# Thresholded attention with a gated MLP: scores in row tiles, probabilities turned by VectorE, values in 64x64 tiles

## The chip, the cores and the metric

The kernel runs on one core of a Trainium2 chip. The metric is the device time of one execution in microseconds (us), as the median of several runs. TensorE (PE) multiplies matrices into PSUM, VectorE (DVE), ScalarE (ACT) and GpSimd (POOL) work on elements, and SyncE (SP) issues all transfers.

## The reference

Eight batches of eight heads, 576 positions, 64 elements per head. Each row of scores keeps only what lies within tau (0.02) of its maximum; the result of attention goes, with heads side by side, through a gated MLP.

```python
scores = scale * np.matmul(q, k.transpose(0, 1, 3, 2))
thresh = np.max(scores, axis=-1, keepdims=True) - tau
scores = np.where(scores >= thresh, scores, -1000000000.0)
scores = scores - np.max(scores, axis=-1, keepdims=True)
attn = np.exp(scores)
attn = attn / (np.sum(attn, axis=-1, keepdims=True) + 1e-09)
x = np.matmul(attn, v)                      # then (B, S, H * D)
...
h = gelu(x @ w_in)                          # 512 -> 1024, halves u and v
v_s = np.einsum('ts,bsd->btd', w_sg, layernorm(v) * g_ln) + b_sg[None, :, None]
out = x + (u * v_s) @ w_out
```

## The kernel before

The unit of work is a pair of heads, n = 0 to 31, four pairs to a batch. In SBUF the two heads of a pair lie on partitions 0 to 63 and 64 to 127. The 576 query rows of a head are four tiles of 128 and a tail of 64; the two tails of a pair share one tile (i = NM = 4). So a pair has nine tiles of scores, each 128 rows by 576 columns in two PSUM banks.

Scores are wanted more exactly than one pass of the f32r form gives, so q and k are split in a high part and a rest (`hi_part`, L590; the rests at L595 and L624). DMAs inside SBUF (`k_place` L608, `k_place_lo` L616, `q_place` L630) then stack these parts on all 128 partitions, so that one full matmul of 288 columns adds two products at once (`scores`, L692): 4 matmuls per tile, 6 for the tail tile. Pair 0 has no split: its scores run in f32, two heads side by side as 64-row tiles of the array (`whole_scores`, L674).

For each tile DVE takes the negative maximum (`maxima`, L701), POOL the threshold (L707), ACT Exp out of PSUM (`exponentials`, L727), and DVE multiplies that by "score at least threshold" and sums the row on the way (`select`, L734). Then the tile of probabilities has to be turned, since values contract over keys. From pair 4 on, tiles i = 0 and 1 of both heads are turned in 32x32 squares by DVE (`turn_squares`, L830), written to DRAM in one transfer (`sqd`, L835) and read back in four (L840). All other tiles, and all tiles of pairs 0 to 3, are turned by PE against an identity (L415, for the tail L879 with `both`), and ACT copies them from PSUM into place (L870, L890, L892).

Values (`values`, L907) run in f32, which the profile counts as two passes per matmul, for 256 query columns (p = 0) and 320 (p = 1): per part five key tiles for each head, into the partitions of that head, as two column tiles 128x64 of the array. DVE multiplies by the reciprocals of the row sums (L916), ACT and POOL split the result for the MLP (L921, L923, L925). The reciprocals are spread through DRAM too (`ird`, L768 to L781).

The MLP's matmuls (L1017, and L1033 for batch 0) lie between those of the pairs. Every step is a function in a list, `plan`; the table `ORDER` gives the sequence in which the steps are issued, and so the sequence on each engine and in SP's one queue of transfers. `PLACES` gives the PSUM bank for each use. Buffers are named by tags: a tag with a number is one buffer that is used again once its last reader is done.

## Time and profile before

| | us |
|---|---|
| median of 3 runs (923.26 to 924.45) | 923.83 |
| span of the profiled execution | 919.5 |
| PE busy | 894.3 (97%) |
| DVE busy | 736.1 (80%) |
| ACT busy | 586.3 (64%) |
| POOL busy | 584.3 (64%) |
| DMA, 172.10 MB | 65.6% of 16 engines on SP's queue |

The span runs from the first to the last instruction of the profiled execution; 4.3 us of the median lie outside of it. A row of a group says how many instructions of one line there are, how long they were busy together, the mean of one in ns, and the idle time of the engine ahead of them with what ended it. Matmuls are pipelined: the mean of one is longer than the distance from one start to the next, and so prices of matmuls are read from start to start in the timeline.

### The profile page before, as it was taken

To read this page: it belongs to the slowest core of one execution; us is meant where nothing else is said; L and a number is where in the kernel's file an instruction comes from. 1 tells how busy PE (TensorE), PEld (TensorE's weight loads), DVE (VectorE), ACT (ScalarE), POOL (GpSimd) and SP (SyncE) were. 2 spreads that over 40 slices of the span, in tenths; PEclk is the share of its full clock that TensorE was granted. 3 is DMA by queue.
4 is the path that set the end of the run, shared out by engine and by line. 5 is a ranking of instruction groups with operands and counts; after the bars stand their busy time and mean duration, and the time that the engine had idled before them with its cause. 6 is when DMAs were issued, how large, how long until landed. Compare 5 with 4: busy or idle time off the path is not lost.

```text
span 919.5 us, 19187 instructions
## 1 busy us (share of the span) xinstructions
PE 894.3 (97%) x6281; PEld 761.4 (83%) x6281; DVE 736.1 (80%) x1605; ACT 586.3 (64%) x1197; POOL 584.3 (64%) x1095
## 2 busy tenths in 40 slices
PE   8989887999999999999999999999999999999998
PEld 5657675889788988988789888888889888899898
DVE  6987999877988779887898679977798778876254
ACT  5787767656676477754685557665686647763361
POOL 5476777656775487655685667764686557754373
PEclk9999989999999999999999999999999999999999
DMA  7776567686866776777767687676777776554001
GB/s 235 207 199 187 157 175 204 193 243 201 233 195 192 210 212 195 213 212 204 218 166 221 189 248 197 187 217 187 217 197 199 216 220 205 150 166 143 20 1 59
DMA packets 93981, 172.10 MB, mean 187 GB/s; under 512 B 25401, under 2 KB 41529, under 8 KB 90298
## 3 DMA queue, kind: packets, MB, share of 16 engines
q1 hardware_dynamic: 93882, 170.88, 65.6%
q8 instruction: 50, 0.82, 0.4%
q14 instruction: 49, 0.40, 0.2%
HBM read 80.61 MB, written 43.48 MB: 135 GB/s over the span
## 4 chain that ended last, share of the span: by engine, by line
PE 74%; DVE 11%; issue 4%; ACT 3%; DMA 3%; POOL 2%; SPq 2%; DVEq 0%; POOLq 0%; ACTq 0%
PE all_banks L1017 40%; PE all_banks L692 14%; PE all_banks L907 12%; PE all_banks L415 7%; DVE nm L701 3%; DVE p L734 3%; DVE sq L830 1%; ACT p L727 1%; DMA rk<-in_kT 1%; DMA ir<-ird 1%; ACT pt L870 1%; DVE gt L1002 1%; DMA klz<-klo 1%; POOL ot L1232 1%; PE all_banks L879 0%
## 5 line engine op out<-in xcount | busy, mean ns | idle before, releaser
L727 ACT ACTIVATE p<-all_banks,nm 128x576 f32<-128x576 f32 x256 | 186.1, 739 | 114.2 <-DVE nm L701 113.0
L701 DVE TENSOR_REDUCE nm<-all_banks 128x1 f32<-128x576 f32 x288 | 210.0, 745 | 45.3 <-PE all_banks L692 37.5
L734 DVE SCALAR_TENSOR_TENSOR p<-all_banks,nm,p 128x576 f32<-128x576 f32 x256 | 203.2, 808 | 39.3 <-ACT p L727 21.2
L692 PE MATMUL all_banks<-ks,qst 128*128 128x288 f32 x620 | 174.4, 314 | 6.0 <-DVE p L734 4.0
L707 POOL TENSOR_TENSOR nm<-columns,nm 128x1 f32<-128x1 f32 x288 | 57.8, 207 | 161.0 <-DVE nm L701 138.1
L907 PE MATMUL all_banks<-pt,rv 128*64 128x256 f32 (+1 forms) x1152 | 151.5, 408 | 0.0
L692 PE MATMUL all_banks<-klz,qst 128*128 128x288 f32 x496 | 138.3, 296 | 0.0
L692 PEld LDWEIGHTS all_banks<-ks,qst 128*128 128x128 f32 x620 | 113.6, 189 | 27.2 <-DVE p L734 15.1
L907 PEld LDWEIGHTS all_banks<-pt,rv 128*64 128x64 f32 x1152 | 77.8, 137 | 54.3 <-issue 5.9
L870 ACT ACTIVATE pt<-all_banks 128x512 f32<-128x512 f32 (+1 forms) x208 | 102.5, 534 | 19.0 <-PE all_banks L415 17.8
L1232 POOL TENSOR_TENSOR ot<-ot,x 128x288 f32<-128x288 f32 x112 | 90.6, 811 | 35.2 <-ACT ot L1241 30.3
L1017 PE MATMUL all_banks<-wsh,z 128*128 128x288 f32 (+2 forms) x512 | 111.8, 298 | 0.3 <-DVE ir L916 0.3
L1017 PE MATMUL all_banks<-x,wi 128*128 128x288 f32 (+2 forms) x720 | 111.7, 299 | 0.0
L415 PE MATMUL all_banks<-ident_r,p 128*128 128x128 f32 x648 | 98.4, 278 | 11.0 <-DVE p L734 8.2
L1017 PE MATMUL all_banks<-wi,x 128*128 128x512 f32 (+1 forms) x424 | 108.8, 401 | 0.0
L1017 PE MATMUL all_banks<-gh,wo 128*128 128x288 f32 (+1 forms) x480 | 106.0, 299 | 0.1
L1017 PEld LDWEIGHTS all_banks<-x,wi 128*128 128x128 f32 x720 | 99.7, 188 | 2.7 <-issue 0.9
L692 PEld LDWEIGHTS all_banks<-klz,qst 128*128 128x128 f32 x496 | 94.0, 189 | 1.0
L415 PEld LDWEIGHTS all_banks<-ident_r,p 128*128 128x128 f32 x648 | 77.4, 143 | 20.5 <-DVE p L734 9.9
L1017 PEld LDWEIGHTS all_banks<-wi,x 128*128 128x128 f32 (+1 forms) x424 | 75.5, 186 | 18.4 <-issue 0.9
L1017 PEld LDWEIGHTS all_banks<-wsh,z 128*128 128x128 f32 x512 | 84.5, 189 | 2.9 <-DVE uu L996 1.1
L830 DVE STREAM_TRANSPOSE sq<-p 128x512 f32<-128x512 f32 (+1 forms) x112 | 82.0, 757 | 0.4
(201 smaller groups left out, 1719.8 us busy)
## 6 DMA issues: line engine op xcount, KB each, us to landing
sqd<-sq SPq DMA_DIRECT2D x28, 1152.0 KB
pt<-sqd SPq DMA_DIRECT2D x112, 288.0 KB
rk<-in_kT SPq DMA_DIRECT2D x32, 320.0 KB
rv<-in_vP SPq DMA_DIRECT2D x32, 320.0 KB
ks<-khi SPq DMA_DIRECT2D x62, 160.0 KB
rq<-in_qT SPq DMA_DIRECT2D x32, 288.0 KB
qst<-qhi SPq DMA_DIRECT2D x62, 144.0 KB
qst<-rq SPq DMA_DIRECT2D x62, 144.0 KB
```

Of the source, the lines that this page charges most:

```text
L415: nc.tensor.transpose(out, x, ident_r.bitcast(F32))
L692: nc.tensor.matmul(sc[:, a, 0:HALF], w, x, start=(j == 0), stop=(j == len(terms) - 1))
L701: nc.vector.tensor_reduce(nmax, st["s", h, i][:, :, 0:HALF], AX.XY, ALU.max, negate=True)
L707: nc.gpsimd.tensor_tensor(thr, toff, st["nm", h, i], ALU.subtract)
L727: nc.scalar.activation(target(h, i), st["s", h, i][:, :, 0:HALF], AF.Exp, bias=st["nm", h, i])
L734: nc.vector.scalar_tensor_tensor(dst, st["s", h, i][:, :, 0:HALF], st["thr", h, i], dst, ALU.is_ge, ALU.mult, accum_out=st["l", p][:, c:c ...
L830: nc.vector.transpose(st["sqt"][:, i, :, m0:m1], src)
L870: nc.scalar.activation(dst, src, AF.Copy)
L907: nc.tensor.matmul(acc[h * D:(h + 1) * D, 0:w], st["v"][:, o:o + D], x, start=(kt == 0), stop=(kt == NM))
L1002: put("stt1", end, lambda: nc.vector.scalar_tensor_tensor(t["tmp"], t["tmp"], GELU_C, t["acc"], ALU.add, ALU.mult))
L1017: nc.tensor.matmul(st["acc"][0:rows[0]] if rows else st["acc"], w, x, start=(j == 0), stop=(j == n - 1))
L1232: return lambda: nc.gpsimd.tensor_tensor(o(), o(), x[b, m][:, ts_], ALU.add)
```

## The change

Six things change together.

1. Scores: for tiles 0 to 3 every pair multiplies the two heads as two 64-row tiles of the array, three products (qh·kh, qh·kl, ql·kh) instead of a stack. That is 12 matmuls for two tiles and 48 per pair. The tail keeps 6 full matmuls, against `qz`, which holds both heads' tails with zeros between. The DMAs that stacked q and k are gone.
2. Select: ACT takes max(s − thr, alpha·(s − thr)) with alpha = BIG (Prelu, from PSUM), then Exp in place in SBUF, with the row sums as a by-product. DVE has no select; POOL makes the threshold and the bias of Exp for two heads in one small operation each.
3. Turning: DVE turns all nine tiles in 32x32 blocks. PE's transposes and ACT's copies are gone, from pair 0 on.
4. Exchange: blocks keep one half where they are; the other goes through DRAM and comes back on other partitions: three puts and three gets for tiles 0 and 1 (u = 0, pieces of 512 bytes), and again for the rest (u = 1, 640 bytes).
5. Values: 64x64 tiles of the array, 9 chunks of keys x 2 heads x 2 halves of rows, 128 columns for u = 0 and 160 for u = 1, into two banks. The result is scaled in two operations for all 576 columns and split in one each.
6. Reciprocals go out in three transfers and come back in four; v is loaded in another layout, 576 KB per pair instead of 320; there are ten buffers for single tiles of probabilities instead of two for double ones and `pm`; `ORDER` and `PLACES` are new. The MLP's own functions change only in how they are entered into the plan.

```diff
-                        terms = [(q[h][:, qo:qo + P], k[:, ko:ko + HALF]) for k in (st["ks", h], st["kl", h])]
...
+                terms = [("q", "k")] if whole_s else [("qh", "kh"), ("qh", "kl"), ("ql", "kh")]
+                for j, (q, k) in enumerate(terms):
+                    for a in range(2):
+                        for h in range(2):
+                            rows = slice(h * D, (h + 1) * D)
+                            nc.tensor.matmul(st["s", h, i][:, a, 0:HALF], st[q][rows, i * P:(i + 1) * P],
+                                             st[k][rows, a * HALF:(a + 1) * HALF], start=(j == 0), stop=(j == len(terms) - 1))
...
-                nc.scalar.activation(target(h, i), st["s", h, i][:, :, 0:HALF], AF.Exp, bias=st["nm", h, i])
...
-                nc.vector.scalar_tensor_tensor(dst, st["s", h, i][:, :, 0:HALF], st["thr", h, i], dst,
-                                               ALU.is_ge, ALU.mult, accum_out=st["l", p][:, c:c + 1])
...
+            tag = slot("p", PBUFS)
...
+                nc.scalar.activation(halves(st["p", h, i]), st["s", h, i][:, :, 0:HALF], AF.Prelu,
+                                     bias=columns_of(i)[1][:, h:h + 1], alpha=BIG)
...
+            return lambda: nc.scalar.activation(st["p", h, i], st["p", h, i], AF.Exp, bias=columns_of(i)[2][:, h:h + 1],
+                                                accum_out=l_of[part][:, c:c + 1])
...
+        def turn_blocks(h, i):
+            def f():
+                u = 0 if i < 2 else 1
+                t, w = turned(u).rearrange("p c e w -> p (c e) w"), WIDTHS[u] // 2
+                if i == NM:
+                    out = t.rearrange("p j (h w) -> p j h w", h=2)[:, :, :, w - HB:w]
+                else:
+                    out = t[:, :, h * w + i % 2 * BLK:h * w + (i % 2 + 1) * BLK]
+                nc.vector.transpose(out, st["p", h, i].rearrange("p (j x) -> p j x", x=BLK))
...
+        def put_blocks(u, k):
...
+                to, rows, e = ((slice(0, 2 * BLK), MIDDLE, 0), (slice(2 * BLK, 3 * BLK), FIRST, 1), (FINAL, FINAL, 1))[k]
+                nc.sync.dma_start(st["sw", u][to].rearrange("p (c w) -> p c w", c=PAIRS), turned(u)[rows, :, e])
...
+        def get_blocks(u, k):
...
+                nc.sync.dma_start(turned(u)[rows, :, e], st["sw", u][src].rearrange("p (c w) -> p c w", c=PAIRS))
...
+                for c in range(PAIRS):
+                    for h in range(2):
+                        for r in range(2):
+                            rows = slice(r * D, (r + 1) * D)
+                            nc.tensor.matmul(st["acc"][h * D:(h + 1) * D, r, :, c0:c0 + w], v[rows, c, h],
+                                             turned(u)[rows, c, :, h * w:(h + 1) * w], start=(c == 0), stop=(c == PAIRS - 1))
```

The order on three engines, in the middle of the program. Numbers at the end of a name tell buffers apart.

On PE before, the scores of a tile (L692) lie among products of the MLP (L1017) and the transposes of tiles that were finished earlier (L415, L879):

```order
L692 MATMUL all_banks<-ks_0_4039,qst_116 128x288
L692 MATMUL all_banks<-klz_123,qst_116 128x288
L692 MATMUL all_banks<-ks_0_4039,qst_116 128x288
L692 MATMUL all_banks<-klz_123,qst_116 128x288
L415 MATMUL all_banks<-ident_r,p_3_4118 128x128 x5
L879 MATMUL all_banks<-both,pm 128x64
L415 MATMUL all_banks<-ident_r,pm 128x128 x4
L1017 MATMUL all_banks<-wi_357,x_3018 128x512 x3
```

On PE after, the scores of a row tile of both heads (L592), both values groups of the pair before (L715), and the next pair's first scores:

```order
L592 MATMUL all_banks<-kh_3507,qh_3580 128x288 x4
L592 MATMUL all_banks<-kl_3590,qh_3580 128x288 x4
L592 MATMUL all_banks<-kh_3507,ql_3745 128x288 x4
L715 MATMUL all_banks<-pt_10_3651,rv_3804 64x2x64 x36
L715 MATMUL all_banks<-pt_10_3755,rv_3804 64x2x80 x36
L592 MATMUL all_banks<-kh_3831,qh_3869 128x288 x4
L592 MATMUL all_banks<-kl_3896,qh_3869 128x288 x4
L592 MATMUL all_banks<-kh_3831,ql_3898 128x288 x4
L809 MATMUL all_banks<-wi_412,x_3389 128x512 x3
```

No transposes stand between any more, and the two values groups follow each other.

On ACT before, Exp (L727) and the copies of turned tiles (L870, L890) take turns with splits and the MLP:

```order
L727 ACTIVATE p_2_4053<-all_banks,nm_1_2_4078 128x576
L727 ACTIVATE pm<-all_banks,nm_0_4_4081 128x576
L1241 ACTIVATE ot_1_0_4116<-all_banks 128x288
L727 ACTIVATE p_3_4118<-all_banks,nm_1_3_4114 128x576
L870 ACTIVATE pt_1_4138<-all_banks 128x4x128
L727 ACTIVATE p_3_4118<-all_banks,nm_0_3_4128 128x576
L921 ACTIVATE x_4141<-ir_0_3809 128x256
L890 ACTIVATE tt_4200<-all_banks 128x128
L870 ACTIVATE pt_1_4138<-all_banks 128x4x128
L921 ACTIVATE x_4141<-ir_1_3900 128x320
```

On ACT after, a Prelu (L628) and an Exp (L634) per tile:

```order
L628 ACTIVATE p_1_0_4188<-all_banks,columns 128x576
L628 ACTIVATE p_0_0_4190<-all_banks,columns 128x576
L1026 ACTIVATE ot_1_0_4198<-all_banks 128x288
L543 ACTIVATE kh_4217<-rk_4041 128x576
L628 ACTIVATE p_0_1_4219<-all_banks,columns 128x576
L634 ACTIVATE p_0_0_4190,l_120<-p_0_0_4190,columns 128x576
L628 ACTIVATE p_1_1_4233<-all_banks,columns 128x576
L634 ACTIVATE p_1_0_4188,l_120<-p_1_0_4188,columns 128x576
L634 ACTIVATE p_1_1_4233,l_120<-p_1_1_4233,columns 128x576
L634 ACTIVATE p_0_1_4219,l_120<-p_0_1_4219,columns 128x576
```

Both tiles of a head pair are selected before the first of them is exponentiated; the copies are gone.

In SP's queue before, the placing transfers of the next pair (L608, L616, L630) lie between the square put (L835) and its gets (L840):

```order
L835 DMA sqd_1943<-sq_1904 128x2304
L608 DMA ks_1_2061<-khi_1977 64x640 x2
L608 DMA ks_0_2064<-khi_1977 64x576 x2
L616 DMA klz_123<-klo_2015 64x576
L584 DMA rq_2068<-in_qT 128x576
L840 DMA pt_0_2070<-sqd_1943 32x4x576
L616 DMA klz_124<-klo_2015 64x576
L768 DMA ird_1_2155<-ir_1_2102 4x32x32
L768 DMA ird_0_2157<-ir_0_2105 4x32x32
L584 DMA rk_2159<-in_kT 128x640
L840 DMA pt_0_2070<-sqd_1943 32x4x576
```

In SP's queue after, the puts of the second part (`swb`, L695), the reciprocals' puts (L656), the gets of the first part (`swa`, L702) and of the second:

```order
L695 DMA swb_2660<-pt_7_2609 288x1x160
L695 DMA swb_2660<-pt_7_2609 576x1x160
L695 DMA swb_2660<-pt_7_2609 288x1x160
L656 DMA ird_2686<-ir_2680 32x32
L702 DMA pt_7_2518<-swa_2641 32x9x128
L702 DMA pt_7_2518<-swa_2641 64x9x128
L656 DMA ird_2686<-ir_2680 32x32
L702 DMA pt_7_2518<-swa_2641 32x9x128
L656 DMA ird_2686<-ir_2680 2x32x32
L702 DMA pt_7_2609<-swb_2660 32x9x160
L702 DMA pt_7_2609<-swb_2660 64x9x160
L702 DMA pt_7_2609<-swb_2660 32x9x160
```

The gets of both parts now stand directly behind the puts of the second part and among the reciprocals.

## Rows read from the trace of the kernel before

**Rows 1.** The page: busy time, the chain that ended last, one group

```profile
PE 894.3 (97%) x6281; PEld 761.4 (83%) x6281; DVE 736.1 (80%) x1605; ACT 586.3 (64%) x1197; POOL 584.3 (64%) x1095
...
PE 74%; DVE 11%; issue 4%; ACT 3%; DMA 3%; POOL 2%; SPq 2%; DVEq 0%; POOLq 0%; ACTq 0%
...
L870 ACT ACTIVATE pt<-all_banks 128x512 f32<-128x512 f32 (+1 forms) x208 | 102.5, 534 | 19.0 <-PE all_banks L415 17.8
```

**Rows 2.** Windows: stretch, its us, PE, PEld, DVE, ACT, POOL, PE clock, DMA, GB/s

```profile
80.00:120.00 40.00, 36.48 (x235) 28.54 (x234) 37.93 (x79) 28.79 (x55) 28.09 (x49) 0.96 0.61 175
240.00:360.00 120.00, 119.90 (x860) 103.05 (x859) 100.10 (x218) 80.03 (x163) 80.52 (x153) 1.00 0.75 211
```

**Rows 3.** Windows, the matmuls of L907 alone: us, PE, PEld, PE clock, DMA, GB/s

```profile
240.00:360.00 120.00, 23.32 (x180) 12.19 (x180) 1.00 0.75 211
```

**Rows 4.** Groups by form on PE: count, busy us, mean ns, idle before

```profile
L415 PE MATMUL all_banks<-ident_r,p 128*128 128x128 f32 x648 | 98.4, 278 | 11.0 <-DVE p L734 8.2 <-ACT tt L890 1.3 <-DVE pm L734 0.9
```

**Rows 5.** Timeline of PE (start, us, instruction, count): four transposes

```profile
408.20 0.60 PE L415 MATMUL all_banks<-ident_r,p 128*128 128x128 f32 x4
408.56 0.38 PE L1017 MATMUL all_banks<-gl,wo 128*128 128x288 f32 x1
408.77 0.43 PE L1017 MATMUL all_banks<-gh,wo 128*128 128x288 f32 x2
409.04 0.30 PE L1017 MATMUL all_banks<-gl,wo 128*128 128x288 f32 x1
```

**Rows 6.** Timeline of PE: the scores of a row tile in pair 0

```profile
16.16 1.24 PE L674 MATMUL all_banks<-rk,rq 64*128 64x288 f32 x8
17.33 0.66 PE L415 MATMUL all_banks<-ident_r,p 128*128 128x128 f32 x4
```

**Rows 7.** Timeline of PE: both values groups of pair 0

```profile
22.80 2.38 PE L907 MATMUL all_banks<-pt,rv 128*64 128x256 f32 x20
25.11 0.48 PE L1261 MATMUL all_banks<-warm 128*128 128x256 f32 x1
...
36.68 2.37 PE L907 MATMUL all_banks<-pt,rv 128*64 128x320 f32 x16
38.88 0.71 PE L907 MATMUL all_banks<-tt,rv 128*64 128x320 f32 x4
```

**Rows 8.** Timeline of PE, cut from 23.05 to 23.064, and to 23.073

```profile
22.80 0.44 PE L907 MATMUL all_banks<-pt,rv 128*64 128x256 f32 x2
...
22.80 0.65 PE L907 MATMUL all_banks<-pt,rv 128*64 128x256 f32 x4
```

**Rows 9.** Timeline of PE: the last score ahead of a values group

```profile
416.21 0.29 PE L692 MATMUL all_banks<-klz,qst 128*128 128x288 f32 x1
416.43 1.30 PE L907 MATMUL all_banks<-pt,rv 128*64 128x320 f32 x8
```

**Rows 10.** Groups by form on DVE: count, busy, mean ns, idle before

```profile
L701 DVE TENSOR_REDUCE nm<-all_banks 128x1 f32<-128x576 f32 x288 | 210.0, 745 | 45.3 <-PE all_banks L692 37.5 <-ACT pt L870 3.0 <-PE all_banks L674 2.2
L734 DVE SCALAR_TENSOR_TENSOR p<-all_banks,nm,p 128x576 f32<-128x576 f32 x256 | 203.2, 808 | 39.3 <-ACT p L727 21.2 <-POOL nm L707 13.0 <-ACT tt L890 1.3
L830 DVE STREAM_TRANSPOSE sq<-p 128x640 f32<-128x640 f32 x56 | 45.4, 822 | 0.4
L830 DVE STREAM_TRANSPOSE sq<-p 128x512 f32<-128x512 f32 x56 | 38.5, 693 | 0.0
```

**Rows 11.** Timeline of ACT: two Exp one behind the other

```profile
241.68 0.73 ACT L727 ACTIVATE p<-all_banks,nm 128x576 f32<-128x576 f32 x1
242.31 0.74 ACT L727 ACTIVATE pm<-all_banks,nm 128x576 f32<-128x576 f32 x1
```

**Rows 12.** Groups by form on ACT: an operation with two pointers

```profile
L1126 ACT ACTIVATE vv<-vv,bn 128x512 f32<-128x512 f32 x32 | 25.9, 809 | 5.4 <-POOL bn L1122 5.4
```

**Rows 13.** Timeline of SyncE's DMA queue: a square put and the gets behind it

```profile
833.92 0.33 SPq L835 DMA_DIRECT2D sqd<-sq  x1
838.05 1.74 SPq L840 DMA_DIRECT2D pt<-sqd  x4
```

More of the change, by code (lines that the diff above doesn't have):

```diff
@@ L508, in weights, with from_single @@
         for k, job in enumerate(jobs):
-            group = (f"w{sum(k >= first for first in (NC, 2 * NC, 2 * NC + NM + 2))}", "first")
-            job(lambda kind, time, fn, group=group: at(kind, time, fn, group), 1.0 + 1.9 * k, k)
-    def from_single(src, hi, lo, put, time, k):
+            job(lambda kind, fn, k=k: at(kind, k, fn), k)
+    def from_single(src, hi, lo, put, k):
         t, sp = {}, spare()
@@ L1101, in new @@
                 return st["v", i]
-            gelu2(put, end, acc, new, f"{b}_{i}", i == NM, part)
+            gelu2(put, acc, new, f"{b}_{i}", i == NM, part)
             def stats():
```

715 lines of the change are left out of this document (258 added, 457 removed), and 445 rows, old and new, of the table ORDER.

## The prediction, on record before the changed kernel ran

> **What bounds the kernel now.** I read the page first: TensorE (PE) is busy for 894.3 of 919.5 us and holds 74% of the chain that ended last; VectorE (DVE) comes next with 80% busy and 11% of the chain [rows 1]. Then the windows, to see whether one limit holds throughout. From 240 to 360 us PE is busy for 119.90 of 120 us, at the full granted clock, with DVE at 100.10, ScalarE (ACT) at 80.03, GpSimd (POOL) at 80.52 and the DMA engines at 0.75. From 80 to 120 us PE has 36.48 of 40, but DVE 37.93: there the first pairs wait for DVE [rows 2]. 180 passes of values lie in those 120 us, 40 to a pair: 4.5 pairs, 26.7 us each [rows 3]. A busy share says nothing of how densely matmuls follow each other, so I went on to start-to-start times. Pricing all matmuls of that stretch by the times below gives about 115.5 of 120 us, so 0.965 of a steady stretch is work that a removed matmul gives back. The time is therefore predicted as PE work removed per pair (n from 8 to 31), DVE work removed in the start, and a look at who might become late instead.
>
> **PE, removed.** Row tiles 0 and 1 of each pair from n=4 on already go by the square exchange; the others still take 22 transposes per pair, all 648 with one shape [rows 4]. From 408.20 to 408.77 us lie four of them and one product; two products take 0.27 us (408.77 to 409.04), so 0.135 each, and the four take 0.435, or 0.109 each [rows 5]. 22 x 0.109 = 2.40, with two passes of L879 as long as a product (0.16 together, an estimate): **2.56 us per pair** gone.
>
> **PE, scores.** 38 full matmuls of 288 columns become 48 half-height ones and 6 full ones. If the two heads' row tiles run side by side, the 48 take 24 slots, together 30: 8 x 0.135 = **1.06 us** gone. Row tiles do run so in pair 0, which already has them: eight f32 passes of 288 columns take 16.16 to 17.33, 0.146 each or 0.51 ns per column [rows 6], close to the 0.43 to 0.45 of the column tiles below, of which two run at once.
>
> **PE, values.** Today: 20 passes of 256 columns from 22.80 to 25.11, 2.31 us, and 20 of 320 columns at (38.88 − 36.68)/16 = 0.1375, 2.75 us; 5.06 per pair [rows 7]. They run as two column tiles at once: a cut of the timeline from 23.05 to 23.064 shows two passes, one to 23.073 four, so both partners of the next slot start within 9 ns [rows 8]. Afterwards there are 72 passes of 128 columns and 72 of 160, in four 64x64 tiles. If four run at once, that is 18 slots of each kind. A slot of 128 columns is half of what two column tiles take for 256 (0.231/2 = 0.1155), one of 160 is 0.1375: 18 x 0.253 = 4.55, **0.5 us** gone.
>
> **PE, added.** Where PE changes between full array and tiles, it loses something: 416.21 to 416.43 is 0.22 for a score before values, against 0.135 [rows 9]; about 0.09 per change. Counted in the order of both kernels, the changed one has 8.9 such changes per pair, the old one 3.4: **0.5 us** more. Net 2.56 + 1.06 + 0.5 − 0.5 = 3.62 per pair; 24 pairs give 87, by 0.965 **90 us**.
>
> **DVE and the start.** Per pair DVE loses nine selects (0.808) and four long transposes (two at 0.822, two at 0.693), and gains nine transposes of 576 columns, between those two, 0.757: 9 x (0.745 + 0.808) + 3.03 = 17.0 becomes 9 x (0.745 + 0.757) = 13.5 [rows 10]. For pairs 4 to 7, where DVE is the limit, that is 4 x 3.5 = 14, of which I take 13 as the tile work beside it has pitches somewhat shorter than these durations; pairs 0 to 3 have no long transposes now and change little, 2. Sum: 90 + 13 + 2 = **105 us** off the profiled execution.
>
> **ACT.** It takes over the select: per tile a Prelu from PSUM and an Exp in place of one Exp from PSUM, of which two follow each other after 0.63 us [rows 11]. Neither new form is in this trace. For the Prelu I take the same 0.63. For the Exp in place, with its sum: at least 0.63 too, at most 0.81, what 512 columns with two pointers take [rows 12]; I take 0.78, near the upper row, since it also has two pointers. In the steady stretch ACT is busy 80.03 / 4.5 = 17.8 per pair; nine Exp go from that (5.7) and the placing of transposed tiles (102.5 over 32 pairs, 3.2) [rows 1 to 3], nine times 1.41 = 12.7 comes: 21.6. PE will need 26.7 − 3.62 / 0.965 = 22.9. ACT stays hidden, but by little more than one us, and becomes the second engine in place of DVE. POOL loses the select's zeros and gains the two-column steps; it stays near 580.
>
> **The exchange.** The placing copies of k and q (1.5 MB per pair) and the square exchange go; the new one moves 2.65 MB per pair in pieces of 512 and 640 B, six puts and six gets. One 1152 KB put now lands 838.05 − 833.92 = 4.1 us after its issue, and four gets take 1.74 us to issue [rows 13]. A pair's last chain, score to values, is then: two maxima 1.5, two Prelu 1.26, two Exp 1.56, two transposes 1.51, three puts at 0.33 and 4.1 to land, three gets 1.3 and at most 4.1 to land: 16.3 us, some of it overlapped, but without queueing. In the changed order the PE work between a pair's last score and its second values group, priced by the rows above, is mostly 17 to 20 us (14.3 at the least). So it fits, with a thin margin; cost taken: nothing. If queueing adds more, PE, which works in order, waits at the values: 1 us per pair costs about 28 over the pairs from 4 on.
>
> **Sum.** 919.5 − 105 = 814.5. The median of 923.83 lies 4.3 above the span, and I keep that: **819 us**.
>
> **Rivals.**
> (a) The exchange is late. SP issues all transfers in one queue; a get that waits for its put also holds the loads behind it. For it: the margin of a few us, where a put issued behind a waiting get adds its whole wait. Against: ten of today's placing transfers per pair leave the same queue. At 2 us per pair 819 + 56 = 875; from 3.7 us per pair the gain is gone and it ends above 923.
> (b) Four 64x64 tiles don't run at once. Each pass brings its own small weights; if PE can feed only two tiles at a time, four passes take as long as two slots one after the other, and values cost 9.1 instead of 4.55: +4.55 x 31 / 0.965 = 146, **965 us**, slower than before. It decides from where four passes cost over 1.7 times a slot: 105 us are 3.3 per pair. Against it: partners start within a few ns of each other [rows 8]. The Trainium skill, "TensorE: Matmul & The Clock Gate", section "Wait — 56ns, not 53.3ns?", says that with hardware decode off each MATMUL costs some 62 ns of its sequencer. By that rule four passes would need 0.248 us for a slot of 0.1155, 36 x 0.248 = 8.9 us per pair (an estimate), and the time would be near 960. The trace speaks against that rule here, since two matmuls that start within 9 ns cannot each have taken 62 [rows 8].
> (c) The row tiles of the scores don't overlap, so that the change doesn't do what it says there: +24 x 0.135 = 3.24 per pair, 819 + 27 x 3.24 / 0.965 = 910 if the first five pairs hide it, as DVE does now.
> (d) ACT becomes the bound. For it: by the sum above it has 1.3 us per pair to spare. It decides from Prelu and Exp together at 1.41 + 1.3 / 9 = 1.55 us per tile, which the upper ends, 0.63 + 0.81, don't reach; at 1.7 it gives 9 x 0.15 x 27 = 36 more, 855.
> (e) The short pieces make the DMA engines the bound. Bytes fall, pieces multiply; at half of today's rate 2.65 MB cost 19 us, and with the loads some 24, over PE's 22.9: 819 + 27 x 1.1 = 849.
> (f) Better than the sum: the changes of mode cost less, PE's waits for DVE shrink: 778.
>
> **How the numbers follow.** Forecast 0.53 (789 to 847, within 1 us of lateness per pair), (f) 0.06, (a) 0.20 of which 0.05 above 923, (b) 0.06, (c) 0.04, (d) 0.07, (e) 0.04. The range goes from 784, below which half of (f) lies, to 890: it leaves out (b), most of (c), the end of (a), together no more than 0.2. Slower by over 0.2% (about what this measurement can tell from no change): (b) 0.06 and (a) 0.05, 0.11; within 0.2%: 0.01; faster: 0.88.
>
> **What the profile of the changed kernel would show.** Right: PE still above 95% in the middle and the largest part of the chain; eighteen slots of values in about 2.1 and 2.5 us; twelve score matmuls of a row tile in 0.8 us; DVE near 610 and ACT near 700 busy; no wait of the values on transfers above half a us. Wrong: PE idle before the values with a DMA as releaser (a); a values group of 36 program matmuls above 4 us (b); twelve scores in 1.6 us (c); Prelu and Exp above 1.55 us per tile (d); 512 B pieces at half the rate (e).

## The result and the profile after

The changed kernel takes **914.55 us** (median of 4 runs, 914.04 to 916.05), the one before, run beside it, 924.01 us: ratio 0.990, 95% interval 0.989 to 0.992. It is faster, but by 9.5 us where 105 were forecast, and it lies outside the range of 784 to 890. The profiled execution has a span of 914.3 us.

The page of the kernel after: busy time, the clock granted to TensorE in 40 slices, the chain that ended last.

```profile
PE 827.9 (91%) x9260; PEld 717.7 (78%) x9260; DVE 644.7 (71%) x1142; ACT 684.5 (75%) x1425; POOL 598.2 (65%) x1053
...
PEclk9897989999989999999899999999999999999999
...
PE 40%; POOL 16%; DVE 12%; DMA 11%; SPq 9%; ACT 8%; issue 6%; DVEq 0%; POOLq 0%; ACTq 0%
```

Against [rows 1], PE has lost 66 us of busy time and is still at 91%, but it holds 40% of the chain instead of 74%: the rest is shared by five others, none above 16%. Windows of the kernel after (stretch, its us, PE, PEld, DVE, ACT, POOL, PE clock, DMA, GB/s), the same stretches as [rows 2]:

```profile
80.00:120.00 40.00, 35.47 (x421) 28.88 (x422) 32.35 (x52) 30.53 (x61) 23.80 (x38) 0.86 0.78 205
240.00:360.00 120.00, 109.77 (x1214) 97.11 (x1215) 84.76 (x153) 92.60 (x193) 83.06 (x149) 0.96 0.60 159
```

In the middle PE is no longer always busy, its clock is below 1.00, and yet no other engine is busy for more than 0.77 of the stretch (ACT). That is what has to be explained.

**The matmuls did get cheaper, about as the prediction had it.** Timeline of PE after: twelve scores of a row tile between products, then the two values groups of a pair, and both groups of another pair without a wait between them (707.78, one row of 144 passes).

```profile
422.77 0.29 PE L809 MATMUL all_banks<-gh,wo 128*128 128x288 f32 x1
422.99 0.54 PE L592 MATMUL all_banks<-kh,qh 64*128 64x288 f32 x4
423.36 0.43 PE L592 MATMUL all_banks<-kl,qh 64*128 64x288 f32 x4
423.62 0.43 PE L592 MATMUL all_banks<-kh,ql 64*128 64x288 f32 x4
423.98 0.53 PE L809 MATMUL all_banks<-gh,wo 128*128 128x288 f32 x2
424.35 0.30 PE L809 MATMUL all_banks<-gl,wo 128*128 128x288 f32 x1
...
426.84 2.19 PE L715 MATMUL all_banks<-pt,rv 64*64 64x128 f32 x72 [0.24 <-ACT p L628]
431.12 3.89 PE L715 MATMUL all_banks<-pt,rv 64*64 64x160 f32 x72 [2.09 <-DMA pt<-swb]
434.94 2.52 PE L809 MATMUL all_banks<-wi,x 128*128 128x512 f32 x8
...
707.78 4.64 PE L715 MATMUL all_banks<-pt,rv 64*64 64x128 f32 x144
712.35 0.40 PE L809 MATMUL all_banks<-wsh,z 128*128 128x288 f32 x1
```

Twelve scores take 422.99 to 423.98, 0.99 us; one by one they would take 12 x 0.135 = 1.62. The row tiles overlap. 72 passes of 128 columns take 2.19 us to the end of the last; both groups together take 4.57 us from start to start (707.78 to 712.35), where 4.55 were forecast: four tiles run at once.

The changes of mode cost more than was forecast. Six slots of two scores would take 0.80 us at 0.133, not 0.99; the product ahead of them takes 0.22, and the two products behind them 0.37 (423.98 to 424.35), where two take 0.27. Over all full matmuls of 288 columns, from start to start and as medians: 0.133 among themselves, 0.223 for the last one ahead of tiles, 0.238 for the first one behind them, in the trace of before as in that of after. So a change costs 0.09 us ahead of it and 0.10 behind it. The prediction, which read only the first [rows 9], took 0.09 in all.

The second values group at 431.12 shows what else went wrong. It starts after 2.09 us without work, for a transfer, and then takes 3.82 us to the next start; the same group takes 2.6 in most other places. After the pause the clock had fallen.

To see where the time went I priced every matmul of both traces by the median start-to-start distance of its shape and successor, and sorted what is left: gaps longer than that by over 0.15 us are waits, half of the time under a granted clock below 0.9 is clock (these are my sums over all matmuls, of the span to the last one, in us).

| kernel | matmuls | waits | low clock | rest | sum |
|---|---|---|---|---|---|
| before | 848.5 | 28.1 | 3.1 | 34.2 | 914.0 |
| after | 746.8 | 93.7 | 26.9 | 37.1 | 904.5 |
| difference | −101.7 | +65.6 | +23.8 | +2.9 | −9.5 |

So about 100 us of PE work are gone, 66 came back as waits and 24 as matmuls at a lower clock. (The border between matmuls and rest depends on how the distances are taken; together they fall by 99.) A coarser count shows the same exchange in the five steady batches alone: time in which PE is not idle, at full clock, falls from 107.3 to 97.1 us per batch, idle time rises by 6.5 and the lower clock costs 2.6, which leaves 1.2 us gained per batch. By stage, from the end of the last values of each batch: the first two batches took 215.5 us before and 221.2 after; the next five 107.5 each before and 106.3 after; the eighth 105.8 and 106.8; what follows the last values 60.8 and 54.8.

**The place of the waits in a steady batch is the turn**, the stretch after a batch's last values, in which the z and x of the MLP (LayerNorm units) are made. Timeline of PE, then ACT, then POOL, then DVE, after the values of the fourth batch ended at 435.0:

```profile
445.83 0.30 PE L601 MATMUL all_banks<-kh,qzl 128*128 128x288 f32 x1
448.90 0.39 PE L592 MATMUL all_banks<-kh,qh 64*128 64x288 f32 x1 [2.77 <-ACT p L628]
450.23 0.84 PE L592 MATMUL all_banks<-kh,qh 64*128 64x288 f32 x3 [0.94 <-ACT p L628]
...
451.96 3.25 PE L809 MATMUL all_banks<-x,wi 128*128 128x288 f32 x12
455.01 1.69 PE L809 MATMUL all_banks<-wi,x 128*128 128x512 f32 x4
```

```profile
446.21 0.61 ACT L796 ACTIVATE gt<-gt 128x512 f32<-128x512 f32 x1
446.74 0.57 ACT L781 ACTIVATE gt<-all_banks 128x512 f32<-128x512 f32 x1
447.21 0.62 ACT L923 ACTIVATE z<-vv 128x512 fp32r<-128x512 f32 x1
448.10 0.74 ACT L628 ACTIVATE p<-all_banks,columns 128x576 f32<-128x576 f32 x1 [0.27 <-POOL columns L614]
```

```profile
445.71 1.27 POOL L917 TENSOR_TENSOR vv<-vv,g_bc 128x512 f32<-128x512 f32 x1
446.96 0.19 POOL L902 TENSOR_SCALAR bn<-bn 128x1 f32<-128x1 f32 x1
447.23 0.55 POOL L906 TENSOR_TENSOR bn<-bn,columns 128x1 f32<-128x1 f32 x1
447.77 0.30 POOL L614 TENSOR_SCALAR columns<-columns 128x2 f32<-128x2 f32 x1
```

```profile
445.47 1.39 DVE L610 TENSOR_REDUCE columns<-all_banks 128x1 f32<-128x576 f32 x2
```

PE wants a PSUM bank for the next scores. It comes free when Prelu (L628) has read the scores in it. Prelu stands on ACT behind gelu and z (L796, L781, L923) and then waits for the threshold (L614), which stands on POOL behind the LayerNorm's gain (L917) and its small steps, although the maxima it needs were done at 446.86. PE, whose next matmul in the program needs that bank, stands for 2.77 us, and afterwards twelve products of 288 columns take 451.96 to 455.01, 0.254 each against 0.135 at full clock. Windows of this stretch after, and of the corresponding one before:

```profile
445.70:456.40 10.70, 6.99 (x32) 5.76 (x31) 8.87 (x15) 10.25 (x21) 10.20 (x20) 0.68 0.17 44
```

```profile
441.70:452.30 10.60, 10.60 (x62) 7.77 (x62) 10.37 (x23) 7.07 (x12) 6.70 (x16) 1.00 0.71 175
```

Before, PE has scores, a values group and products of the MLP for the whole stretch; after, ACT and POOL are full (10.25 and 10.20 of 10.70), and what is next in PE's order needs them. In the 10.70 us just ahead of this stretch, and in those ahead of a batch's last values, the same engines of the kernel after have room, and means over 120 us hide it:

```profile
435.00:445.70 10.70, 10.70 (x62) 8.41 (x62) 8.64 (x16) 6.40 (x12) 4.72 (x9) 0.96 0.63 178
531.40:542.10 10.70, 10.13 (x185) 8.64 (x185) 3.60 (x5) 5.77 (x13) 1.95 (x6) 1.00 0.67 187
```

PE's largest waits over the span by what ended them (total us, times, longest):

```profile
PE all_banks L592 <- ACT p L628: 19.4, 28, 2.8
PE all_banks L715 <- DMA pt<-swb: 10.8, 12, 2.1
PE all_banks L592 <- DMA rk<-in_kT: 5.7, 1, 5.7
PE all_banks L809 <- DVE uu L788: 5.7, 4, 1.9
```

### The profile page after: what moved, and what is told of

It is laid out like the page before. It is cut to its first block, busy times and chain, and to the rows that moved or that the text cites. A ratio compares the mean times of both kernels' runs of the same rounds, so it can differ in the third digit from the quotient of the medians.

```text
span 914.3 us, 24350 instructions
## 1 busy us (share of the span) xinstructions
PE 827.9 (91%) x9260; PEld 717.7 (78%) x9260; DVE 644.7 (71%) x1142; ACT 684.5 (75%) x1425; POOL 598.2 (65%) x1053
## 3 DMA queue, kind: packets, MB, share of 16 engines
q1 hardware_dynamic: 207170, 150.17, 60.8%
## 4 chain that ended last, share of the span: by engine, by line
PE 40%; POOL 16%; DVE 12%; DMA 11%; SPq 9%; ACT 8%; issue 6%; DVEq 0%; POOLq 0%; ACTq 0%
PE all_banks L809 23%; PE all_banks L715 8%; PE all_banks L592 7%; DMA pt<-swb 4%; SPq L702 3%; DVE pt L685 3%; DVE columns L610 3%; POOL vv L917 3%; ACT p L628 2%; DMA ir<-ird 2%; POOL z L930 2%; SPq L656 2%; ACT p L634 2%; DMA ird<-ir 2%; SPq L695 2%
## 5 line engine op out<-in xcount | busy, mean ns | idle before, releaser
L610 DVE TENSOR_REDUCE columns<-all_banks 128x1 f32<-128x576 f32 x288 | 205.8, 744 | 79.4 <-PE all_banks L592 67.1
L628 ACT ACTIVATE p<-all_banks,columns 128x576 f32<-128x576 f32 x288 | 202.6, 736 | 69.0 <-POOL columns L614 68.4
L685 DVE STREAM_TRANSPOSE pt<-p 128x576 f32<-128x576 f32 x288 | 206.0, 752 | 48.5 <-PE all_banks L715 35.5
L634 ACT ACTIVATE p<-p,columns 128x576 f32<-128x576 f32 x288 | 220.8, 770 | 3.1 <-POOL columns L618 1.5
L715 PE MATMUL all_banks<-pt,rv 64*64 64x128 f32 (+1 forms) x4608 | 165.8, 293 | 15.8 <-DMA pt<-swb 10.8
L715 PEld LDWEIGHTS all_banks<-pt,rv 64*64 64x64 f32 x4608 | 148.2, 137 | 30.1 <-issue 14.8
L614 POOL TENSOR_SCALAR columns<-columns 128x2 f32<-128x2 f32 (+1 forms) x160 | 54.4, 340 | 135.8 <-DVE columns L610 132.5
L592 PE MATMUL all_banks<-kh,qh 64*128 64x288 f32 x496 | 80.2, 355 | 23.8 <-ACT p L628 19.4
L1017 POOL TENSOR_TENSOR ot<-ot,x 128x288 f32<-128x288 f32 x112 | 90.5, 815 | 10.5 <-ACT ot L1026 8.9
L592 PEld LDWEIGHTS all_banks<-kh,qh 64*128 64x128 f32 x496 | 44.5, 187 | 57.0 <-ACT p L628 33.2
L809 PEld LDWEIGHTS all_banks<-gh,wo 128*128 128x128 f32 x480 | 78.7, 188 | 5.2 <-issue 3.0
L809 PE MATMUL all_banks<-wsl,z 128*128 128x288 f32 (+2 forms) x256 | 76.2, 302 | 0.0
L809 PE MATMUL all_banks<-gl,wo 128*128 128x288 f32 (+1 forms) x240 | 69.5, 296 | 0.0
L592 PE MATMUL all_banks<-kh,ql 64*128 64x288 f32 x496 | 58.6, 294 | 0.1
```

Of the source, the lines that this page charges most:

```text
L592: nc.tensor.matmul(st["s", h, i][:, a, 0:HALF], st[q][rows, i * P:(i + 1) * P], st[k][rows, a * HALF:(a + 1) * HALF], start=(j == 0), stop ...
L610: return lambda: nc.vector.tensor_reduce(nm, st["s", h, i][:, :, 0:HALF], AX.XY, ALU.max, negate=True)
L614: return lambda: nc.gpsimd.tensor_scalar(nt, nm, toff, 1.0, ALU.subtract, ALU.mult)
L628: nc.scalar.activation(halves(st["p", h, i]), st["s", h, i][:, :, 0:HALF], AF.Prelu, bias=columns_of(i)[1][:, h:h + 1], alpha=BIG)
L634: return lambda: nc.scalar.activation(st["p", h, i], st["p", h, i], AF.Exp, bias=columns_of(i)[2][:, h:h + 1], accum_out=l_of[part][:, c:c ...
L685: nc.vector.transpose(out, st["p", h, i].rearrange("p (j x) -> p j x", x=BLK))
```

## Experiments

All ratios are to the kernel before, run beside each (922.65 to 923.60 us), with 95% intervals. Differences in us are to the 914.55 of the kernel after, or to the kernel that is named.

**e1: the exchange left out.**

```diff
-                nc.sync.dma_start(st["sw", u][to].rearrange("p (c w) -> p c w", c=PAIRS), turned(u)[rows, :, e])
...
-                nc.sync.dma_start(turned(u)[rows, :, e], st["sw", u][src].rearrange("p (c w) -> p c w", c=PAIRS))
```

> The changed kernel without the exchange: the six puts and six gets of each pair are left out, so the values multiply what VectorE has turned, wherever it lies, and the output is not the reference's. If the exchange (its landing and its places in SyncE's queue) is what TensorE waits for, most of the 66 us of added waits and the 24 us of added slow clock go: about 840 us. If the way from the maximum over GpSimd to ScalarE and back to the PSUM banks is the cause, or ScalarE's load, 895 us or more.

895.0 us, 0.971 (0.968 to 0.974). The exchange costs 19.6 us, not nothing, but that is a fifth of the 95.5 that are missing to the forecast. In the trace of e1 PE still waits 19.7 us in 26 pieces for L628.

**e2: threshold and bias moved from POOL to DVE, behind the maxima.**

```diff
-            return lambda: nc.gpsimd.tensor_scalar(nt, nm, toff, 1.0, ALU.subtract, ALU.mult)
...
+                    nc.vector.tensor_scalar(nt, nms, toff, 1.0, ALU.subtract, ALU.mult)
+                    nc.vector.tensor_tensor(tm, nms, nt, ALU.subtract)
```

> The two small operations that make threshold and bias of a tile move from GpSimd to VectorE, right behind the tile's last maximum; nothing is left out. If the detour through GpSimd's queue between maximum and Prelu is the cause, 870 to 885 us and ScalarE's idle time ahead of Prelu (69 us) falls by more than half. If the exchange or ScalarE's load is the cause, 905 to 920.

971.3 us, 1.053 (1.051 to 1.055): both expectations wrong, and slower than the kernel after. DVE's busy time grew from 644.7 to

```profile
PE 845.5 (87%) x9260; PEld 726.4 (75%) x9260; DVE 761.4 (79%) x1462; ACT 685.4 (71%) x1425; POOL 519.1 (54%) x733
```

so 320 small operations added 117 us, 0.365 each on average. The average hides two kinds: 215 of them take 0.20 us on average, the other 105 take 0.83. Of these 105, 99 began while POOL was in an operation and ended within 0.04 us of its end; of the 215 only 14 were done while the POOL operation beside them still ran. From 443.9 us, one of POOL and one of DVE:

```profile
443.99 1.40 POOL L549 TENSOR_TENSOR kl<-rk,kh 128x576 fp32r<-128x576 f32 x1
444.14 1.26 DVE L616 TENSOR_TENSOR columns<-columns 128x2 f32<-128x2 f32 x1
```

So some 67 of the 117 us are DVE standing beside POOL and not work. What couples the two engines is not shown here. e2 therefore traded one wait for another and doesn't test the detour through GpSimd by itself. The 117 us on DVE cost 57 us of time, half, at a mean DVE share of 79%: here a mean share below 80% was no room.

**e3 and e4: only one of ACT's two passes.** In e3 the Exp reads PSUM in Prelu's place, without a threshold; in e4 only the Prelu stays.

```diff
-                nc.scalar.activation(halves(st["p", h, i]), st["s", h, i][:, :, 0:HALF], AF.Prelu,
-                                     bias=columns_of(i)[1][:, h:h + 1], alpha=BIG)
+                nc.scalar.activation(halves(st["p", h, i]), st["s", h, i][:, :, 0:HALF], AF.Exp,
+                                     bias=columns_of(i)[0][:, h:h + 1], accum_out=l_of[part][:, c:c + 1])
```

> Leaves the threshold out: Exp reads PSUM at the Prelu's place with the maximum from VectorE as its bias, and the second operation on ScalarE is gone, so ScalarE loses 220 us and waits no longer for GpSimd. If ScalarE's load or the detour through GpSimd is the cause, 860 us or less. If the exchange is the cause, 900 or more.

> Leaves Exp out: the Prelu stays with its bias from GpSimd, the second operation on ScalarE is gone (220 us of load) and with it the row sums. If ScalarE's load is the cause, about as fast as the kernel with Exp alone, 860 to 870. If the detour through GpSimd is the cause, 900 or more while Exp alone is at 870 or less. If the exchange is the cause, 900 or more.

909.1 us (0.986, 0.984 to 0.989) and 913.7 us (0.990, 0.988 to 0.991). ACT has 186 and 211 us less to do, and that brings 5.4 and 0.9 us. ACT as the one bound is out, and so is the wait for POOL's threshold by itself, which e3 doesn't have.

**e5: the LayerNorm's gain and the low part of z left out on POOL.**

```diff
-                nc.gpsimd.tensor_tensor(st["v", i], st["v", i], g_bc[0:rows], ALU.mult)
...
-                    nc.gpsimd.tensor_tensor(st["zl", i], st["v", i], st["zh", i], ALU.subtract)
```

> Leaves out two GpSimd operations of 1.3 us in each full unit of the layer norm: the gain, and the rest of z, for which the high part is read once more. That is 64 operations, about 82 us of GpSimd. The waits of the changed kernel lie mostly in some 40 us at the turn of each batch, where the layer norm goes through GpSimd. If GpSimd's part of it is what TensorE waits for there: 875 us or less. If the way into it is (last values, reciprocals, split of x) or the exchange: 895 or more.

900.6 us, 0.977 (0.971 to 0.982): 14 us, with runs from 897 to 908. In the profiled one, which is among the shortest, the span is 19.1 us below that of after: 9.4 in the five batches (104.4 instead of 106.3 each), 3.7 in the start, 3.8 in the eighth batch, 2.2 behind it.

**e6, e7, e10: single links of the turn.** Three buffers instead of two for the LayerNorm units (and nine for P); Exp's bias a constant; the MLP's entry on the third pair's x instead of the fourth's.

```diff
-                    pool, w, tag = mtmp, FH, f"mt{i % 2}"
+                    pool, w, tag = mtmp, FH, f"mt{i % 3}"
...
-            return lambda: nc.gpsimd.tensor_tensor(tm, nm, nt, ALU.subtract)
+            return lambda: None
...
-            return lambda k, c: (xh_of, xl_of)[k][b, c][:, ts_]
+            return lambda k, c: (xh_of, xl_of)[k][b, min(c, 2)][:, ts_]
```

> Three buffers in place of two for a unit of the layer norm, paid for with one of the ten buffers for probabilities; nothing is left out. If units wait for the buffer that GpSimd frees last: 890 us or less. If not, 905 to 920; the missing buffer of probabilities can only make it slower.

> The bias of Exp is the constant minus tau for all rows, so the second small GpSimd operation of each tile goes (160 operations, 32 us of GpSimd); the result differs only by rounding. If GpSimd's queue is the bound at the turn of a batch: 895 to 905 us. If not: 911 to 916.

> The MLP reads the third pair's x where it should read the fourth's, so it doesn't wait for the last pair of its batch (values, reciprocals, scaling, split on ScalarE and GpSimd); all work stays. If the way into the MLP is what the turn of a batch waits for: 880 us or less. If the layer norm behind it or ScalarE's and GpSimd's queues are: 900 or more.

917.8 us (0.994, 0.992 to 0.996), 917.2 (0.994, 0.991 to 0.996), 915.9 (0.992, 0.989 to 0.994): nothing gained, all three as the kernel after or 1 to 3 us above it. None of these links holds the turn by itself.

**e8: e1, e3 and e5 together.**

> Three causes away together: no exchange, Exp alone on ScalarE without a threshold, no gain and no rest of z in the layer norm (the parts of the three kernels that left these out one at a time). If the added waits stand on these three, and each alone is masked by the others: 820 to 840 us, the sum of the prediction. If it is the order of work alone (TensorE's list has nothing to do at the turn of a batch): 860 or more.

869.1 us, 0.942 (0.940 to 0.943): 45.4 us, more than the 19.6 + 5.4 + 13.9 = 38.9 of the three alone. By its expectation that speaks for the order of work alone. It doesn't decide: e14 below has the same order and takes 831.6 us.

**b1 and e9: only PE's work changed.** The third term of the scores is left out, 16 full matmuls per pair or 66 us of PE work, in the kernel before (b1); in the one after (e9) the second and third are, 16 slots per pair, as much by the same price. This tests the step on which the whole prediction stands, that PE work removed is time given back.

```diff
-                        terms = [(q[h][:, qo:qo + P], k[:, ko:ko + HALF]) for k in (st["ks", h], st["kl", h])]
+                        terms = [(q[h][:, qo:qo + P], k[:, ko:ko + HALF]) for k in (st["ks", h],)]
...
-                terms = [("q", "k")] if whole_s else [("qh", "kh"), ("qh", "kl"), ("ql", "kh")]
+                terms = [("q", "k")] if whole_s else [("qh", "kh")]
```

> The kernel before with less work on TensorE: the second of the two stacked terms of the scores is left out for the eight full tiles of each pair, 16 matmuls of 0.133 us, 2.1 us per pair and 66 us over 31 pairs; all transfers stay. If removed TensorE work comes back as the prediction took it (by 0.965), about 860 us. If other waits stand close behind it in this kernel already, 885 to 905.

> The changed kernel with the same 2.1 us per pair less on TensorE: only qh times kh is left of the three products of the row tiles (8 of 12 matmuls per tile pair left out). If TensorE is still the bound, about 850 us. If the start and the turns of the batches wait for other chains, only the dense parts can give something: 885 to 905.

906.6 us (0.982, 0.980 to 0.984) and 905.3 us (0.981, 0.979 to 0.983), both just above the second expectation. Of 66 us the kernel **before** gives back 17, 0.26; the kernel after 9, 0.14 (0.17, if one takes the 56 us by which matmuls and rest fell in its own trace). b1 in the middle of the program, and a wait of PE over the span, first in before and then in b1:

```profile
240.00:360.00 120.00, 116.80 (x796) 95.51 (x798) 100.95 (x223) 81.09 (x169) 81.01 (x156) 1.00 0.75 211
```

```profile
PE all_banks L692 <- DVE p L734: 4.0, 5, 2.6
...
PE all_banks L692 <- DVE p L734: 11.5, 22, 2.9
```

PE has 8.2 us per batch less to do, a batch is shorter by 1.8, and PE now waits for banks that DVE's select (L734) frees.

**e11: another order.** `ORDER` and `PLACES` of the kernel after replaced by tables that a replay of the traced durations found shorter.

```diff
-    160 16 162 17 18 161 41 163 19 165 166 167 176 42 178 177 168 43 44 170 179 173 169 184 246 61 215 193 181 45 216
...
+    160 16 162 244 14 12 31 246 17 18 61 161 13 3 7 11 8 9 10 4 2 0 6 5 165 245 166 167 19 168 163 1 15 176 177 178 247
```

> The same operations in another order: the tables ORDER and PLACES are replaced by ones found by many small exchanges of neighbours, judged by replaying the durations of this kernel's trace through five queues. If the order at the start and the turns holds back the gain: 895 to 905 us. If the loads of the engines do, whatever the order: 912 or more. An order with the MLP half a batch later wasn't tried by these small exchanges.

936.9 us, 1.016 (1.013 to 1.018), 22 us slower than the kernel after. The replay misjudged it; a better order was not found, and whether there is one stays open.

**b3 and b2: the kernel before without row maxima and threshold,** alone (b3) and with b1's edit (b2). DVE is 182 us lower, POOL 47.

```diff
-                nc.vector.tensor_reduce(nmax, st["s", h, i][:, :, 0:HALF], AX.XY, ALU.max, negate=True)
...
-                nc.gpsimd.tensor_tensor(thr, toff, st["nm", h, i], ALU.subtract)
+                st["thr", h, i] = toff
```

> The kernel before without the row maxima and the threshold made from them (Exp and the selection take a constant; 288 reductions on VectorE and as many small operations on GpSimd left out, VectorE about 206 us lower by the row of the reductions). Theory A (TensorE bounds the kernel before, VectorE is only close behind): little, 905 to 920 us, since TensorE's waits in the kernel before sum to 28 us. Rival B (VectorE is as much a bound as TensorE): under 900 us.

> The kernel before without the row maxima and without the third term of the scores (TensorE 66 us lower, as in b1, and VectorE about 206 us lower). Theory A (VectorE was what stopped b1 at 907): the 66 us come back now, 845 to 865 us. Rival (other chains, ScalarE, GpSimd and the turn of a batch, stop it as well): 875 to 900 us.

b3: 899.9 us, 0.975 (0.973 to 0.976); b2: 860.3 us, 0.931 (0.929 to 0.933). b3 lies at the edge of its rival B ("under 900"), b2 within its theory A. The stages say why b3 is neither clearly: the first two batches end at 200.3 instead of 215.5, while a later batch takes 106.4 instead of 107.5. In the start the work between scores and select was the limit, in the middle PE. Set against b3, the same 66 us of PE work are now worth 39.6, 0.60, and in the middle 6.1 of 8.2 us per batch. The middle of b2, where the room is:

```profile
240.00:360.00 120.00, 118.43 (x848) 100.18 (x847) 79.80 (x192) 82.89 (x172) 78.73 (x118) 1.00 0.77 218
```

So what stopped b1 in the middle was mainly the chain maximum, threshold, select that runs through DVE. Since POOL's threshold goes with the maxima, DVE and POOL are not told apart here.

**e12 to e15: the kernel after, with more and more of the rest out of the way.** e12 leaves out maxima and threshold; e13 the exchange and DVE's transposes from the second pair on; e15 is both; e14 is e15 with e3 and e5.

```diff
-            return lambda: nc.vector.tensor_reduce(nm, st["s", h, i][:, :, 0:HALF], AX.XY, ALU.max, negate=True)
+            return lambda: None
...
-                                     bias=columns_of(i)[1][:, h:h + 1], alpha=BIG)
+                                     bias=toff, alpha=BIG)
...
+            if ("pt", u) not in st and n > 0:
+                st["pt", u] = first_pt[u]
...
+                if n > 0:
+                    return
```

> The kernel after without the row maxima, the threshold and its second column (Prelu and Exp take a constant; VectorE about 206 us lower, GpSimd about 86 us lower, and a bank of scores waits for ScalarE only). Theory A (VectorE and GpSimd between scores and Prelu are what the waits come from): 840 to 865 us. Theory B (several chains of about equal length; exchange, LayerNorm and ScalarE at .95 at the turn remain): 875 to 900 us.

> The kernel after without the exchange and without the transposes on VectorE from the second pair on (the values read the first pair's tile; VectorE about 200 us lower; a tile of P is free as soon as Exp has passed). Theory B (VectorE is one of several chains): 10 to 25 us under e1, as the maxima were worth 23 us: 870 to 885 us. Rival (VectorE was the only other bound): under 860 us.

> The kernel after without the exchange, without maxima and threshold and without the transposes from the second pair on; the LayerNorm units and both passes of ScalarE stay whole. Theory B (GpSimd's LayerNorm and ScalarE's second pass hold it too): 845 to 865 us. Rival (VectorE and the exchange are all): 830 to 838 us, as e14.

> The kernel after without the exchange, with Exp alone in place of Prelu and Exp, without the gain and low part of the LayerNorm units, without maxima and threshold, and without the transposes on VectorE from the second pair on (the values read the first pair's tile): every engine beside TensorE has room. Theory B (the gain on TensorE went into chains through the other engines): TensorE's own 747 us, 37 us between and 25 to 35 us at the start remain, 805 to 825 us. Rival (the order of TensorE's own work holds it): it stays near e8, 850 us or more.

| kernel | us | ratio | two batches end | a later batch |
|---|---|---|---|---|
| after | 914.6 | 0.990 (0.989 to 0.992) | 221.2 | 106.3 |
| e12: no maxima | 891.9 | 0.966 (0.963 to 0.969) | 214.4 | 103.9 |
| e1: no exchange | 895.0 | 0.971 (0.968 to 0.974) | 221.1 | 103.5 |
| e13: e1, no transposes on DVE | 889.7 | 0.963 (0.962 to 0.965) | 217.1 | 102.6 |
| e15: e13, no maxima | 865.1 | 0.937 (0.935 to 0.939) | 203.8 | 101.1 |
| e14: e15, one pass on ACT, less LayerNorm | 831.6 | 0.901 (0.899 to 0.902) | 189.4 | 98.0 |

e12 is as theory B had it, e13 5 us above its theory B, e15 at the upper edge; e14 is 7 us above its. PE's matmuls hardly differ in these (747 us in after, 734 in e14), but waits and clock fall from 121 us to 49. The single steps from the kernel after are worth 22.7 (maxima), 19.6 (exchange), 13.9 (LayerNorm), 5.4 (ACT's second pass) and, on top of e1, 5.3 (transposes): 66.9; together they are worth 82.9. Taking one away lets the next one come late, and the last two, worth 19 when first, are worth 33.5 when last. That is how chains side by side behave, and not one bound. The middle of e14, and the stretch of its fourth turn that corresponds to 445.70 to 456.40 above:

```profile
240.00:360.00 120.00, 117.41 (x1441) 104.72 (x1442) 29.22 (x70) 71.61 (x170) 63.73 (x100) 1.00 0.27 77
...
393.90:404.00 10.10, 7.11 (x39) 5.83 (x38) 3.97 (x10) 8.56 (x20) 4.63 (x14) 0.83 0.02 6
```

The hole in the turn is still there, with DVE at 3.97 and POOL at 4.63 of 10.10 us. PE, then ACT:

```profile
396.46 0.40 PE L592 MATMUL all_banks<-kh,qh 64*128 64x288 f32 x1 [1.97 <-ACT p L629]
```

```profile
394.05 0.63 ACT L801 ACTIVATE gt<-gt 128x512 f32<-128x512 f32 x1
394.59 0.58 ACT L786 ACTIVATE gt<-all_banks 128x512 f32<-128x512 f32 x1
395.07 0.62 ACT L928 ACTIVATE z<-vv 128x512 fp32r<-128x512 f32 x1
395.59 0.73 ACT L629 ACTIVATE p<-all_banks,columns 128x576 f32<-128x576 f32 x1
```

Exp out of PSUM stands behind the same gelu and z as Prelu did, now without maximum or threshold, and PE waits 1.97 us for it instead of 2.77. So most of this wait comes from what is issued ahead of it on ACT, and not from DVE or POOL. A kernel in which only that order is changed was not made, and so its worth is not shown.

## Why the prediction was wrong

- **The step that failed: "0.965 of a steady stretch is work that a removed matmul gives back".** 0.965 was how densely PE was filled. What a removed matmul gives back depends on how far behind the next engine is, and b1 measures that in the very same kernel: 0.26. PE at 119.90 of 120 us and 74% of the chain [rows 1, 2] were read rightly, and PE was the bound of the middle. But a bound with others close behind it gives back only the distance to the next: in b1 DVE does as much in 120 us as before, 100.95 against 100.10, and PE waits for it. The runs show what mattered instead: with the maxima and the threshold gone 0.60 comes back (b2 against b3), with the other engines relieved the kernel after comes to a span of 829.2 (e14). That this is near the forecast's 814.5 is in part luck: its start gains 26 us and its end 9.4, where 15 and nothing were forecast, and a later batch takes 98.0 us where 15.0 less than 107.5, 92.5, were forecast. Nor is it like against like: the kernel before gains by relief too, and without maxima and threshold in both, the change is worth 8.0 us (b3 against e12).
- **PE's terms were right in kind, and their sum was too large.** Values take 4.57 us (4.55 forecast), four tiles at once; the 22 transposes were worth 2.1 us in the steady batches of before, rather than 2.4; and a change of mode costs 0.19 us and not 0.09, which for the 5.5 more per pair that were counted is another 0.55 us. In the steady batches PE's work fell by 2.6 us per pair, by 3.0 in e14, where it waits least; 3.62 were forecast. (8 x 0.135 in the scores is 1.08, not 1.06; that is nothing beside it.) ACT came to 684.5 us (near 700 expected), DVE to 644.7 (near 610). Rivals (b) and (c) are refuted by the rows above. Of the signs that were named, two of those for "right" failed (PE above 95% in the middle: 91%; no wait of the values on transfers above half a us: there are some of up to 2.1), and the first of those for "wrong" came true. The Trainium skill's 62 ns of sequencer per MATMUL ("TensorE: Matmul & The Clock Gate", section "Wait — 56ns, not 53.3ns?") are stated there for hardware decode off; whether it is off here no run shows. In (b) they were applied to passes. The group of 128 columns takes 2.02 us from start to start where the other follows directly, 28 ns for each of 72 passes; counted by the program's 36 matmuls it is 56 ns. So the rows speak clearly against the price that (b) drew, and only slightly against the rule in that other reading.
- **"A look at who might become late" was made on means per pair.** ACT's 21.6 us per pair against PE's 22.9 was sound: Prelu and Exp follow each other in 1.39 us per tile, near the 1.41 assumed. But the new order puts the LayerNorm units where the next scores on PE wait for the same engines, with ACT at 10.25 and POOL at 10.20 of 10.70 us, just after a stretch in which they have 6.40 and 4.72. Rival (d) is wrong as a bound of the whole and right as a stretch; it needed a window of 10 us, not of 120, and a look at what stands ahead of Prelu on ACT there.
- **The exchange, "cost taken: nothing", costs 19.6 us** (e1). Rival (a) had the mechanism, and its price of 28 us per us of lateness; the lateness is about 0.7 us per pair. SP's rows show one part: three puts take 2.10 us to issue and three gets 1.89, 0.70 and 0.63 each, where 0.33 and 0.44 were taken from [rows 13]. Those rows were a quick stretch: over the whole trace of before the median issue takes 0.55 us, after 0.60. The other part is the queue: between these puts and their gets stand issues for the first part and for the reciprocals.

```profile
418.46 2.10 SPq L695 DMA_DIRECT2D swb<-pt  x3
420.66 2.21 SPq L702 DMA_DIRECT2D pt<-swa  x2
...
425.23 1.89 SPq L702 DMA_DIRECT2D pt<-swb  x3
```

 From the first put's issue at 418.46 to the values at 431.12 it is 12.7 us, against 10.5 by the prediction's terms (1.0 + 4.1 + 1.3 + 4.1).
- **The start, "−15", became +5.7.** The first two batches end later than before. The start's limit was not the select alone, which moved from DVE to ACT, but the chain scores, maximum, threshold, select: without maxima and threshold the kernel before gains 15.2 there (b3). In the kernel after that is worth only 6.8 (e12), of 32 with everything relieved (e14); what else holds its start was not separated.
- **The clock was not in the sum.** 24 us more of matmuls at the lower level come with the waits and go with them: 26.9 us in after, 9.4 in e14.
- What the range lacked is a rival "nothing is the bound": each of (a) to (e) made one thing late and left the rest of the gain. Between the two profiled spans (919.5 and 914.3) the start loses 5.7 and the eighth batch 1.1, five batches gain 6.0 and the part after the last values 6.0: 5.2 us. So the sign was luck in part: those last 6.0 us stood in no term of the sum, and without them the two spans would be equal within 1 us. The medians differ by 9.5, and most of the rest is the choice of executions. In the runs that list both, the time is 1.7 to 2.1 us above the span, so that the profiled span of 919.5 belongs to some 921.4 us, 2.6 below the median of 924.01, while that of after belongs to its slowest run, 916.05, 1.5 above its median. So of the 4.3 us that were put outside the span above, and kept in the forecast's sum, about 2 lie outside it.

## What to carry to other kernels

A kernel whose order has been tuned can have several chains of nearly equal length, as this one has, and the busy share of its bound says little about the return of work taken off it (here 97% busy, and 0.26 returned); measure that return first by leaving some of the work out, which takes one run. Judge who is next in windows as short as the program's own stages, not by means over a batch: a mean of .75 on every engine is compatible with PE standing idle in one stage and the others in the next. If several chains are nearly as long as the longest, a change pays in full only when it relieves all of them in the same stretch, as e14 comes near to doing. Whether a new order made around the change would pay is not shown; the one that was tried was slower. Price a change of mode on both of its sides.

## What the runs showed of the hardware that was not expected

- After most of its stands of 2 to 3 us PE's granted clock fell for some us from the higher of its two levels (2.4 GHz) to the lower (1.2 GHz): the granted share was 0.68 over the 10.70 us with the 2.77 us wait, with products at 0.254 us instead of 0.135, and a values group at 3.82 instead of 2.60. Not after all of them: 3.25 us that ended at 150.4 in before and 2.00 us that ended at 832.9 in after left it at the higher level, while in before it fell at 124.8, behind stands of 0.81 and 1.67. The lower level cost 3.1 us in the kernel before and 26.9 in the one after; with 66 us of added waits went another 24.
- A small operation on DVE (two columns) takes 0.20 us on average in two thirds of the cases of e2, and 0.83 in the others, nearly all of which end with an operation of POOL; a maximum over 576 columns takes 0.744.
- A change between full array and tiles of TensorE costs 0.09 us ahead of it and 0.10 behind it (0.223 and 0.238 us from start to start against 0.133).
- Reading the accumulator after Exp takes ACT about 0.1 us between two operations (443.97 to 444.07 in the timeline), which makes an Exp with a row sum 0.76 us instead of 0.67 (medians).
- Four 64x64 tiles do run at once, with a weight load for every pass (9260 of each in the page of after): a slot of 128 columns of f32 takes 0.112 us where the next group follows directly (2.02 us for 18).
